# Moving some swapped copies of h from SyncE's DMA queue to ScalarE's in an attention and gated-MLP kernel

## The chip, the cores and the metric

One NeuronCore of a Trainium2 chip runs the whole kernel. The metric is the device time of one launch in microseconds (us), the median of several runs. The engines are named as the profile names them: PE is TensorE, DVE is VectorE, ACT is ScalarE, POOL is GpSimd, SP is SyncE, which here only issues DMAs. A "q" behind a name (SPq) means the engine's instruction queue, as it waits or issues a DMA.

## The reference

```python
B, S, D, H, F = 1, 2048, 576, 32, 4608     # head size D // H = 18
xn = layernorm(x)
# attention
q, k, v = split_heads(xn @ wqkv)
p = softmax(q @ k.T * 18 ** -0.5)
s = (p @ v merged over the heads) @ wo
# gated MLP without a nonlinearity inside
h = (xn @ w_gate) * (xn @ w_up)
g = silu(h @ w_down)
out = x + s * g
```

All tensors are float32. Products that need accuracy are done on operands split into a high and a low part (float32r), hence three matmuls for one.

## The kernel before

The work has a first phase (layer norm, the projections to q, k and v, which go to DRAM scratch), a long main phase, and a last projection with `wo`. The main phase mixes two kinds of work on PE, in an order that a planner in the program writes out by hand when the kernel is built (`order`, lines 1089 to 1170); every engine then runs its own list in that fixed order.

- **Attention**, head after head, 64 items a head: `a_item` (line 581) makes a block of scores in PSUM bank `pa` (line 588) for the row maxima that DVE takes (line 590); `b_item` (line 614) makes a block of scores in bank `pb` (line 620), and ACT takes its exponential (line 622, `pt<-pb`). `pb` has two buffers, so a score matmul can only start when ACT has finished with the block two before it. `pv_group` (line 631) multiplies by v.
- **The gated MLP**, in 72 units. Unit u is a pair of 128 columns of the hidden size (q, of NF2 = 18 column groups) for one block of 512 rows (c, of 4 passes): u = 18 c + q. PE works in two streams r = 0, 1 that use half of the rows of the array each (lines 667 to 672). Stream 0 makes the up product, which ACT copies out (`us`, line 675); stream 1 makes the gate product, which DVE multiplies by it (line 682). ACT then writes the high part of h (`hs`, line 685) and POOL the low part (line 686). The weights `wgu` and `wd` are loaded raw in the first pass, split by ACT and POOL (lines 190, 191, 223, 224), and stored to scratch by SP (`swg` line 196, `swd` line 229), from which the later passes load them (lines 182, 217).
- **The down product** of unit u (line 712) runs while unit u + 1 is made. Each stream owns 64 partitions, but needs h from all 128, so `turn_round` (line 692) makes a second copy of h with the two halves of the partitions swapped: `hx`, by two DMAs of 512 KB each (line 702). `hx` has one buffer. For unit 0 the copies are issued right behind POOL's part of h (`gate_end`, line 688); for units 1 to 70 in `down_end` (line 750), when the down product of the unit before has read `hx` for the last time; for unit 71 in `gate_end`, in two pieces of two DMAs (`hxl`, 256 KB each), one behind each half of h.

At the last unit of a pass `x_block` (line 357) loads the next 512 rows of x (`xc<-sx`) from scratch. `load_ring` and `load_pair` (lines 244 to 248) bring the heads' q and k as `ring<-sqk` and `pair<-sqk`.

SP issues every DMA named so far, in program order; POOL issues a few others. The DMAs of the hardware queues signal their landing on eight semaphores (DMAHW0 to DMAHW7) that are handed out in turn, and a DMA waits, before it is issued, until the one that used its semaphore before it has landed. A waiting instruction at the head of a queue holds back what stands behind it.

Of the kernel before, what the change touches and what calls it, by code (L numbers as in the profile page):

```python
# [20 lines left out]
FT = mybir.dt.float32  # L21
# [19 lines left out]
def kernel(  # L41
# [10 lines left out]
    nc = tc.nc  # L52
# [7 lines left out]
    NF2 = F // 256  # L60
# [509 lines left out]
    with ExitStack() as mid:  # L570
# [88 lines left out]
        hs, us = {}, {}  # L659
        TERMS = [t for b in range(9) for t in ((b, b, 0), (9 + b, b, 0), (b, b, 1))]  # L660
        half = [slice(0, 64), slice(64, 128)]
# [15 lines left out]
        def gate_end(n, ps):  # L677
            u, j = divmod(n, 2)
            if j == 0:
                hs[u] = gp.tile([128, 2, 2, 512], FR, name="hs", bufs=2)  # L680
            h32 = us.pop(n)
            nc.vector.tensor_tensor(h32, ps, h32, op=OP.mult)  # L682
            g_get(n + 2)
            hj = hs[u][:, j]
            nc.scalar.activation(hj[:, 0, :], h32, AF.Copy)  # L685
            nc.gpsimd.tensor_tensor(hj[:, 1, :], h32, hj[:, 0, :].bitcast(FT), op=OP.subtract)  # L686
            if u == 0 and j or u == len(units) - 1:
                turn_round(u, j)

        hx = {}  # L690

        def turn_round(u, j):

            if u == len(units) - 1:
                if j == 0:
                    hx[u] = accp.tile([128, 2, 2, 512], FR, name="hxl", tag="acc")
                js = slice(j, j + 1)
            else:
                hx[u] = gp.tile([128, 2, 2, 512], FR, name="hx", bufs=1)
                js = slice(0, 2)  # L700
            for r in range(2):
                nc.sync.dma_start(hx[u][half[r], js].bitcast(FT), hs[u][half[1 - r], js].bitcast(FT))

        DTERMS = [(k, j, a, e) for k in range(2) for j in range(2) for a, e in ((0, 0), (0, 1), (1, 0))]

# [25 lines left out]
        def down_end(r, u, s, ps):  # L731
            c, q = units[u]
            cs = slice(r * HALF, (r + 1) * HALF)
            if q == 0 and c >= 2:
                ready(sdone, 4 * c - 8 + s)
            a = sums(4 * c + s)[:, cs]
            if q == 0:
                nc.vector.tensor_copy(a, ps[:, 0:HALF])
            else:
                nc.vector.tensor_tensor(a, a, ps[:, 0:HALF], op=OP.add)  # L740
            if q == NF2 - 1 and c < NCH - 1:
                seen[c, s] = seen.get((c, s), 0) + 1
                if seen[c, s] == 2:
                    silu_store(4 * c + s)
            if s == 3:
                seen[u] = seen.get(u, 0) + 1
                if seen[u] == 2:
                    d_get(u + 1)
                    if u + 1 < len(units) - 1:
                        turn_round(u + 1, 1)  # L750
# [540 lines left out]
```

## Time and profile before

| | us |
|---|---|
| median of 3 runs | 2593.03 |
| lowest and highest of them | 2589.69, 2594.57 |
| the profiled execution | 2593.24 |
| its span, first to last instruction | 2591.4 |
| PE busy | 2573.7 |
| DVE busy | 1918.9 |
| ACT busy | 1459.4 |
| POOL busy | 589.2 |

The profile is a trace of one execution. Times in its views count from the start of the span. In a row of the timeline the first number is the start, the second the length, in square brackets stands how long the engine had been idle before it and what ended that. In a list of waits stand who waited, for what, the sum, the number of times and the longest.

### The profile page before, as it was taken

What the parts mean: (1) busy time and instruction counts of PE and PEld (TensorE: products, weight loads), DVE (VectorE), ACT (ScalarE), POOL (GpSimd) and SP (SyncE); (2) the same over time, 40 slices, a digit from 0 to 9 for tenths busy, and PEclk for the clock granted to TensorE, in tenths of its full rate; (3) what the DMA queues carried; (4) which work ended last, traced back from release to release, by engine and by line L of the source; (5) the groups of instructions that cost most, each with busy time, mean ns of one, the idle gap of its engine ahead of it and who ended that gap; (6) DMA issues with size and microseconds to landing.
All of it is one profiled execution on the core that took longest, in us unless ns stands there. A gap on an engine that the chain in (4) does not pass through costs nothing.

```text
span 2591.4 us, 59097 instructions
## 1 busy us (share of the span) xinstructions
PE 2573.7 (99%) x24360; PEld 2106.9 (81%) x24360; DVE 1918.9 (74%) x3377; ACT 1459.4 (56%) x2688; POOL 589.2 (23%) x659
## 2 busy tenths in 40 slices
PE   8999999999999999999999999999999999999999
PEld 7899877787888888877888888877788888887779
DVE  6208777777778888877788788877788888777527
ACT  5222666666665555655555565655555565555561
POOL 3114444434421111111111111111111211111115
PEclk9999999999999999999999999999999999999999
DMA  7799989888885666665686556655675666665567
GB/s 240 227 277 276 269 225 225 231 214 228 220 200 178 179 180 178 169 181 158 178 193 174 173 163 184 180 159 173 171 195 153 175 183 175 173 177 169 154 181 253
DMA packets 195897, 504.57 MB, mean 195 GB/s; under 512 B 58112, under 2 KB 116352, under 8 KB 156588
## 3 DMA queue, kind: packets, MB, share of 16 engines
q1 hardware_dynamic: 185676, 489.05, 67.8%
q0 software_dynamic: 9952, 11.74, 1.7%
q8 instruction: 192, 3.15, 0.5%
q14 instruction: 77, 0.63, 0.1%
HBM read 312.21 MB, written 107.61 MB: 162 GB/s over the span
## 4 chain that ended last, share of the span: by engine, by line
PE 96%; DMA 1%; DVE 1%; SPq 0%; issue 0%; ACT 0%; POOL 0%; ACTq 0%; POOLq 0%; DVEq 0%
PE pg L670 35%; PE pg L631 17%; PE pg L712 16%; PE pa L588 12%; PE pb L620 9%; PE pg L395 2%; PE pa L341 2%; PE pb L341 2%; PE pg L1221 1%; PE pa L1221 1%; PE pb L1221 1%; DMA hx<-hs 0%; DMA ring<-sqk 0%; DMA xin<-in_A_x_dram 0%; DVE hl L345 0%
## 5 line engine op out<-in xcount | busy, mean ns | idle before, releaser
L590 DVE TENSOR_REDUCE mx<-pa 128x1 f32<-128x512 f32 x2048 | 1361.6, 684 | 159.1 <-PE pa L588 69.7
L622 ACT ACTIVATE pt<-pb 128x512 f32<-128x512 f32 x2048 | 1154.9, 597 | 564.1 <-PE pb L620 458.9
L670 PE MATMUL pg<-xc,wgu 64*128 64x512 f32 x7776 | 1396.7, 392 | 0.0
L670 PEld LDWEIGHTS pg<-xc,wgu 64*128 64x128 f32 x7776 | 1054.9, 186 | 50.4 <-DVE acc L740 0.2
L620 PE MATMUL pb<-pair,ring 56*128 56x512 f32 x2006 | 788.9, 399 | 0.9 <-DMA ring<-sqk 0.9
L588 PE MATMUL pa<-pair,ring 54*128 54x512 f32 x2001 | 784.7, 398 | 0.3 <-DVE mx L590 0.3
L712 PE MATMUL pg<-wd,hs 64*128 64x288 f32 x3408 | 537.2, 292 | 1.2 <-DVE acc L740 1.2
L712 PE MATMUL pg<-wd,hx 64*128 64x288 f32 x3408 | 528.7, 292 | 1.2 <-DMA hx<-hs 1.1
L712 PEld LDWEIGHTS pg<-wd,hs 64*128 64x128 f32 x3408 | 474.1, 186 | 6.0 <-DVE acc L740 1.9
L712 PEld LDWEIGHTS pg<-wd,hx 64*128 64x128 f32 x3408 | 468.0, 185 | 5.7 <-DMA hx<-hs 1.9
L631 PE MATMUL pg<-pt,vt 128*32 128x512 f32 x4096 | 454.8, 594 | 0.0
L686 POOL TENSOR_TENSOR hs<-us,hs 128x512 fp32r<-128x512 f32 x144 | 186.2, 1293 | 1129.8 <-ACT hs L685 1087.9
L588 PEld LDWEIGHTS pa<-pair,ring 54*128 54x128 f32 x2001 | 363.2, 184 | 82.5 <-issue 47.8
L620 PEld LDWEIGHTS pb<-pair,ring 56*128 56x128 f32 x2006 | 364.7, 184 | 12.0 <-ACT us L675 1.5
L631 PEld LDWEIGHTS pg<-pt,vt 128*32 128x32 f32 x4096 | 125.6, 110 | 284.4 <-issue 280.6
L637 DVE TENSOR_TENSOR oc<-oc,pg 128x512 f32<-128x512 f32 x69 | 47.4, 688 | 320.8 <-PE pg L631 320.6
L740 DVE TENSOR_TENSOR acc<-acc,pg 128x288 f32<-128x288 f32 x544 | 233.8, 443 | 27.1 <-PE pg L712 24.2
L685 ACT ACTIVATE hs<-us 128x512 fp32r<-128x512 f32 x144 | 91.0, 632 | 154.3 <-DVE us L682 152.9
L651 POOL DMA_DIRECT2D sot<-oc x124 | 64.1, 523 | 329.7 <-DVE oc L648 327.6
L610 POOL DMA_DIRECT2D pair<-mt x128 | 78.0, 615 | 225.9 <-DVE mt L605 223.8
L635 ACT ACTIVATE oc<-pg 128x512 f32<-128x512 f32 x32 | 19.2, 599 | 189.2 <-PE pg L631 189.2
L191 POOL TENSOR_TENSOR wgu<-wraw,wgu 128x384 fp32r<-128x384 f32 x108 | 108.3, 1015 | 76.0 <-ACT wgu L190 70.9
(130 smaller groups left out, 1376.8 us busy)
## 6 DMA issues: line engine op xcount, KB each, us to landing
wgu<-swg SPq DMA_DIRECT2D x102, 1152.0 KB
hx<-hs SPq DMA_DIRECT2D x142, 512.0 KB
wd<-swd SPq DMA_DIRECT2D x50, 1152.0 KB
swg<-wgu SPq DMA_DIRECT2D x36, 1152.0 KB
pair<-sqk SPq DMA_DIRECT2D x192, 144.0 KB
ring<-sqk SPq DMA_DIRECT2D x384, 72.0 KB
swd<-wd SPq DMA_DIRECT2D x18, 1152.0 KB
sqk<-hl SPq DMA_DIRECT2D x32, 512.0 KB
```

The costliest lines, as they stand in the source:

```text
L191: nc.gpsimd.tensor_tensor(w[:, 9 + b:12 + b, :], raw[:, b:b + 3, :], w[:, b:b + 3, :].bitcast(FT), op=OP.subtract)
L341: nc.tensor.matmul(p, wq[b, a], xcs[c][:, e, :], start=n == 0, stop=n == len(PAIRS) - 1)
L588: nc.tensor.matmul(p, q[rows, t * 128:(t + 1) * 128], k[rows, c * 512:(c + 1) * 512], start=True, stop=True)
L590: nc.vector.tensor_reduce(mx[h][:, t, c:c + 1], p, axis=AX.X, op=OP.max)
L620: nc.tensor.matmul(p, k[rows, t * 128:(t + 1) * 128], q[rows, c * 512:(c + 1) * 512], start=True, stop=True)
L622: nc.scalar.activation(pt[t, c], p, AF.Exp, scale=scale)
L631: nc.tensor.matmul(p[32 * c:32 * c + 32, :], vt[h // 2][:, t, 6 * (h % 2):6 * (h % 2) + 32], pt[t, c], start=t == ts[0], stop=t == ts[-1])
L670: nc.tensor.matmul(ps, gw[n][half[r], a, :], xg[i][half[r], e, :], start=k == 0, stop=k == len(TERMS) - 1)
L685: nc.scalar.activation(hj[:, 0, :], h32, AF.Copy)
L686: nc.gpsimd.tensor_tensor(hj[:, 1, :], h32, hj[:, 0, :].bitcast(FT), op=OP.subtract)
L712: nc.tensor.matmul(ps[:, 0:HALF], (hx if k else hs)[u][half[r], j, a, s * 128:(s + 1) * 128], dw[u][half[r], k, j, e, :], start=n == 0, st ...
L740: nc.vector.tensor_tensor(a, a, ps[:, 0:HALF], op=OP.add)
```

## The change

The two DMAs of `turn_round` are issued on ACT's queue, and not on SP's, for units 0 to 3 and for those units whose place in a pass is the first or the last: 17, 18, 35, 36, 53, 54 and 71 (u % 18 is 0 or 17). That is eleven units and 24 DMAs of 146. Nothing else is edited.

```diff
             for r in range(2):
-                nc.sync.dma_start(hx[u][half[r], js].bitcast(FT), hs[u][half[1 - r], js].bitcast(FT))
+                (nc.scalar if u < 4 or u % NF2 in (0, NF2 - 1) else nc.sync).dma_start(hx[u][half[r], js].bitcast(FT), hs[u][half[1 - r], js].bitcast(FT))
```

PE, DVE and POOL run the same lists as before. Three places on ACT and SP follow, with the semaphores that each instruction waits for; a number behind a name (PE_49) is that of the build. First ACT, before, in unit 3, around 287 us of the profile (`draw` is the raw down weight that becomes `wd`):

```order
L622 ACTIVATE pt<-pb 128x512 [waits PE_49] x2
L223 ACTIVATE wd<-draw 128x2x288 [waits DMAHW3_49,DMAHW2_49,DMAHW5_49,PE_49,Pool_49]
L622 ACTIVATE pt<-pb 128x512 [waits PE_49]
L223 ACTIVATE wd<-draw 128x2x288 [waits DMAHW6_49,DMAHW4_49]
L622 ACTIVATE pt<-pb 128x512 [waits PE_49] x4
```

The same place with the change:

```order
L622 ACTIVATE pt<-pb 128x512 [waits PE_49] x2
L702 DMA hx<-hs 64x2048 [waits DMAHW6_49,DMAHW1_49,DMAHW7_49,PE_49,Pool_49]
L702 DMA hx<-hs 64x2048 [waits DMAHW2_49]
L223 ACTIVATE wd<-draw 128x2x288 [waits DMAHW5_49,DMAHW3_49]
L622 ACTIVATE pt<-pb 128x512 [waits PE_49]
L223 ACTIVATE wd<-draw 128x2x288 [waits DMAHW6_49,DMAHW4_49]
L622 ACTIVATE pt<-pb 128x512 [waits PE_49] x4
```

The pair of DMAs has come to stand ahead of a split of weights and of an exponential.

Next SP with the change, in unit 17, around 746 us: the last loads of x for the next pass (`xc`) and the first of the ring loads that follow them.

```order
L364 DMA xc<-sx 64x1024 [waits DMAHW0_49,PE_49]
L364 DMA xc<-sx 64x1024 [waits DMAHW1_49,PE_49]
L364 DMA xc<-sx 64x1024 [waits DMAHW2_49,PE_49]
L242 DMA ring<-sqk 18x1024 [waits DMAHW3_49]
L242 DMA ring<-sqk 18x1024 [waits DMAHW4_49]
```

ACT at the same place, with the change:

```order
L622 ACTIVATE pt<-pb 128x512 [waits PE_49] x12
L702 DMA hx<-hs 64x2048 [waits DMAHW5_49,DMAHW1_49,DMAHW6_49,PE_49,Pool_49]
L702 DMA hx<-hs 64x2048 [waits DMAHW2_49]
L223 ACTIVATE wd<-draw 128x2x288 [waits DMAHW7_49,DMAHW0_49]
L622 ACTIVATE pt<-pb 128x512 [waits PE_49] x2
```

The copies stood between the `xc` and the ring loads on SP, and are now on ACT with the semaphores DMAHW1 and DMAHW2, which the last two `xc` loads used before them.

Last ACT in unit 71, around 2498 us, with the change:

```order
L685 ACTIVATE hs<-us 128x512 [waits DMAHW2_49,DMAHW1_49,DVE_49]
L702 DMA hxl<-hs 64x1024 [waits DMAHW4_49,Pool_49]
L702 DMA hxl<-hs 64x1024 [waits DMAHW5_49]
L622 ACTIVATE pt<-pb 128x512 [waits PE_49] x8
L675 ACTIVATE us<-pg 128x512 [waits PE_49]
```

Behind ACT's half of h stands now the copy, which waits for POOL's half (Pool_49), and behind that eight exponentials.

The changed program's semaphores give, for each moved pair, the DMAs that must have landed before it is issued, by the turn of the eight:

| unit | first DMA waits for | second DMA waits for |
|---|---|---|
| 0 | `sv<-vo`, long before | `swg<-wgu`, the one before the last |
| 1 | the second of three ring loads | the third of them |
| 2 | the third of three ring loads | the third of three `pair<-sqk` |
| 3 | the first of three `pair<-sqk` | the `swg<-wgu` behind these |
| 17 | the last `xc` load but one | the last `xc` load |
| 18 | a `wgu<-swg` of the unit before | the first of three `pair<-sqk` |
| 35 | the last `xc` load but four | the last `xc` load but two |
| 36 | the second of three `pair<-sqk` | a `wgu<-swg` of the unit before |
| 53 | an `xc` load in the middle | the last `xc` load but five |
| 54 | the last ring load of an earlier group | a `wgu<-swg` of the unit before |
| 71, first half | a ring load of an earlier unit | the next ring load |
| 71, second half | the first half's second DMA | the first `wor<-in_A_wo_dram` |

## The prediction

> **What bounds the kernel now.** I read the page's busy times first, then who PE waits for, then the rows of the copies themselves, and last the timeline at each place where a copy moves.
>
> ```profile
> PE 2573.7 (99%) x24360; PEld 2106.9 (81%) x24360; DVE 1918.9 (74%) x3377; ACT 1459.4 (56%) x2688; POOL 589.2 (23%) x659
> PE pg L712 <- DMA hx<-hs: 1.1, 1, 1.1
> PE pb L620 <- DMA ring<-sqk: 0.9, 1, 0.9
> PEld pg L712 <- DMA hx<-hs: 1.9, 2, 1.5
> L702 SPq DMA_DIRECT2D hx<-hs x142: 467/587/5686, 219.2 to 2483.7; - x142
> L622 ACT ACTIVATE pt<-pb 128x512 f32<-128x512 f32 x2048 | 1154.9, 597 | 564.1 <-PE pb L620 458.9 <-PE pa L588 63.0 <-PE pg L670 16.3
> ```
>
> PE is busy 2573.7 of 2591.4 us, so it sets the end, and what is to be won by earlier copies is what PE loses to them. That is little: its weight loads lose 1.9 us to `hx` in the whole stretch of the first units (the 1.1 us of its matmuls lies inside that), and 0.9 us to a ring load in unit 17, which on SP stands behind the copy of that unit. All gains together are 2.8 us, about 0.1% of the time.
>
> ACT has room on average (56%), but it has a strict order, and its exponentials hand PSUM back to PE. With two `pb` buffers an exponential that ends late by more than the gap to the second next score matmul stops PE, and PE, being busy to 99%, cannot win that back. So each moved pair has to be asked: when does ACT get to go on, and which score matmul is waiting then?
>
> **The change part by part.** A pair of copies holds SP for 1.10 to 1.12 us when nothing else delays it (rows below at 2499.45, 783.57 and 748.90). There is no DMA from ACT in the trace; I take the same 1.1 us for a pair on ACT, some 0.6 us for its second DMA. From below the bound is nothing, from above the 5.7 us of the longest row of L702.
>
> *Unit 71.* The copy stands behind POOL's half of h, which only begins when ACT has ended its half.
>
> ```profile
> 2497.41 0.63 ACT L685 ACTIVATE hs<-us 128x512 fp32r<-128x512 f32 x1 [0.64 <-DVE us L682]
> 2498.12 1.30 POOL L686 TENSOR_TENSOR hs<-us,hs 128x512 fp32r<-128x512 f32 x1 [19.70 <-ACT hs L685]
> 2497.95 2.28 ACT L622 ACTIVATE pt<-pb 128x512 f32<-128x512 f32 x4
> 2498.71 0.39 PE L620 MATMUL pb<-ring,pair 56*128 56x512 f32 x1
> 2499.45 1.10 SPq L702 DMA_DIRECT2D hxl<-hs  x2
> 2509.81 0.39 PE L620 MATMUL pb<-ring,pair 56*128 56x512 f32 x1
> 2510.46 1.10 SPq L702 DMA_DIRECT2D hxl<-hs  x2
> ```
>
> On SP that wait costs nobody. On ACT the exponential that began at 2497.95 comes after the pair: 2499.45 + 1.10 + 0.60 = 2501.15 is its end, and the score matmul that needs its buffer, at 2498.71 before, starts at about 2501.2: **+2.5**. The second half of h repeats it: 2510.46 + 1.10 + 0.60 = 2512.2 against 2509.81, about 2512.3: **+2.5**. Nothing covers these; POOL was idle before, so its 1.30 us cannot come sooner.
>
> *Unit 17.* ACT reaches the pair at about 749, just after the last reading of `hx`, when SP issued it too. But by the table of semaphores the pair waits for the last two `xc` loads.
>
> ```profile
> 745.31 1.54 SPq L364 DMA_DIRECT2D xc<-sx  x2
> 748.90 1.12 SPq L702 DMA_DIRECT2D hx<-hs  x2
> 750.07 5.75 SPq L242 DMA_DIRECT2D ring<-sqk  x6
> 749.03 0.68 ACT L223 ACTIVATE wd<-draw 128x576 fp32r<-128x576 f32 x1
> 749.60 0.59 ACT L622 ACTIVATE pt<-pb 128x512 f32<-128x512 f32 x1
> 750.93 0.39 PE L620 MATMUL pb<-pair,ring 56*128 56x512 f32 x1
> 1334.03 0.45 SPq L364 DMA_DIRECT2D xc<-sx  x1
> 1343.13 0.48 SPq L702 DMA_DIRECT2D hx<-hs  x1
> SPq L702 <- DMA xc<-sx: 0.8, 1, 0.8
> 745.00:756.00 11.00, 11.00 (x106) 10.96 (x104) 10.75 (x21) 9.35 (x18) 5.32 (x6) 1.00 1.06 210
> ```
>
> How long such a load takes is seen in unit 35: the copy at 1343.13 had waited for the `xc` load issued at 1334.03, 9.1 us. The last two of unit 17 were issued at 745.3 and about 746.4, so they land near 754.4 and 755.5. The second copy then goes at 755.5 to 756.1, the split of weights takes the next 0.57 (749.03 to 749.60 before), the exponential 0.6: it ends at 757.3, and the score matmul of 750.93 starts at 757.4, **+6.5**. The ring loads no longer stand behind the copy and have these microseconds besides, so the 0.9 us that PE waited for them is gone: **+5.6** in all. From below: eight loads of 256 KB in flight, 2.1 MB, at the 286 GB/s that the row of unit 3 below shows in place of 210 here take 7.3 us, which makes it +3.8; from above +7.
>
> *Units 0 to 3.* The rows of unit 3 first, with the stretch from 283 to 292 us, whose last columns are PE's clock, the DMA engines' share and the GB/s, and then ACT's idle times in units 0 and 1:
>
> ```profile
> SPq L196 <- DMA swd<-wd: 2.8, 1, 2.8
> 283.30 0.34 SPq L196 DMA_DIRECT2D swg<-wgu  x1
> 283.00:292.00 9.00, 9.00 (x98) 8.86 (x96) 7.38 (x14) 6.33 (x12) 5.29 (x5) 1.00 1.02 286
> 287.54 0.69 ACT L223 ACTIVATE wd<-draw 128x576 fp32r<-128x576 f32 x1
> 288.13 0.58 ACT L622 ACTIVATE pt<-pb 128x512 f32<-128x512 f32 x1
> 290.60 0.39 PE L620 MATMUL pb<-pair,ring 56*128 56x512 f32 x1
> 221.68 0.60 ACT L675 ACTIVATE us<-pg 128x512 f32<-128x512 f32 x1 [2.54 <-PE pg L670]
> 244.52 0.60 ACT L675 ACTIVATE us<-pg 128x512 f32<-128x512 f32 x1 [2.08 <-PE pg L670]
> 263.14 1.09 ACT L622 ACTIVATE pt<-pb 128x512 f32<-128x512 f32 x2
> ```
>
> In units 0 and 1 no exponential runs yet (the first is at 263.14), and ACT idles 2.54 and 2.08 us before its next due work: POOL's 1.3 and 1.1 us of issue in unit 0, 1.1 in unit 1 fit into it. Zero. In unit 3 the second copy waits for the `swg` store issued at 283.30, when `swd` had landed. Ahead of its end stand four `draw` of 144 KB, three `pair` of 144 KB and its own 1152 KB: 2.2 MB, at 286 GB/s 7.7 us, so it lands at 291.0. The DMA engines are full there (share 1.02), so I leave that landing where it was, though a copy of 1 MB has changed queues. The second copy goes at 291.0 to 291.6, split 0.6, exponential 0.6: it ends at 292.8, and the score matmul of 290.60 starts at about 292.9, **+2.3**. Because this is fixed by a landing and not by PE, the 1.9 us that PE no longer waits in unit 2, and any loss there behind a `pair` load, are inside it and not added. Bounds: 0, if the store lands by 288.5, to +4.5.
>
> *Units 35, 18, 36, 53, 54.* In unit 35 the second copy cannot go before 1343.13 on ACT either.
>
> ```profile
> 1341.81 0.60 ACT L622 ACTIVATE pt<-pb 128x512 f32<-128x512 f32 x1 [0.39 <-PE pb L620]
> 1343.66 0.39 PE L620 MATMUL pb<-pair,ring 56*128 56x512 f32 x1
> 783.57 1.12 SPq L702 DMA_DIRECT2D hx<-hs  x2
> 785.67 0.39 PE L620 MATMUL pb<-pair,ring 56*128 56x512 f32 x1
> 1373.39 1.11 SPq L702 DMA_DIRECT2D hx<-hs  x2
> 1375.48 0.39 PE L620 MATMUL pb<-pair,ring 56*128 56x512 f32 x1
> 1938.66 0.60 ACT L622 ACTIVATE pt<-pb 128x512 f32<-128x512 f32 x1 [7.03 <-PE pb L620]
> 1972.67 1.09 ACT L622 ACTIVATE pt<-pb 128x512 f32<-128x512 f32 x2 [2.14 <-PE pg L670]
> ```
>
> 1343.13 + 0.48 + 0.60 = 1344.2, the matmul of 1343.66 starts at 1344.3: **+0.7**. In units 18 and 36 the exponential behind the pair ends at 783.57 + 1.12 + 0.60 = 785.3 and 1373.39 + 1.11 + 0.60 = 1375.1, before 785.67 and 1375.48; in 53 and 54 ACT idles 7.03 and 2.14 us. Zero, and up to 0.5 each if a pair takes ACT half as long again.
>
> The sum: 5.0 + 5.6 + 2.3 + 0.7 = **+13.6 us** on the profiled execution's 2593.24, that is **2606.8**. That execution lies 0.2 us above the median of the runs shown, so I take 2607.
>
> [...]
>
> **The rivals.**
>
> *Not slower: the wait does not hold ACT's computing.* If a DMA that waits on ACT's queue lets the exponentials behind it pass, only the removed waits count: 1.9 and 0.9, so 2590.4. For it: the trace has no DMA on ACT. Against it: on SP the wait does hold the queue (the copy at 1343.13 waited 0.8 us and nothing was issued past it). [...]
>
> *About as before: what a pair waits for lands early.* SP is freed of 24 DMAs and could issue the `xc` loads and the store sooner. Then unit 17 costs only its issue (748.90 + 1.12 + 0.57 + 0.60 = 751.2 against 750.93, +0.4, less 0.9), unit 3 gives its 1.9 us back, unit 35 nothing, and unit 71 its 5.0: +2.6, or 2595.8. Against it: no copy stands ahead of the `xc` loads of unit 17 on SP, and in unit 3 the DMA engines are full.
>
> *Slower still: the issue itself is held.* SP's longest copy held its queue for 5.7 us in the crowded first units. If ACT's is held like this once, at unit 3, the term there grows by about 5.1, to 2611.9; the point from which this decides is an issue of more than 1.1 us on ACT.
>
> **How the numbers follow.** The sum as worked out has 0.67, the held issue 0.13, early landings 0.12, a wait that does not hold ACT 0.08. The low ends of the terms (3.8 for unit 17, 0 for unit 3, 0.3 for unit 35, and 2.8 for unit 71 if the issue costs nothing) make +6.9, or 2600; the high ends (7, 4.5, 1.0, 6 and 2 for the pairs counted as zero) +20.5, or 2614, where the held issue lies too. For 8 in 10 I take 2599 to 2613. Less than 0.2%, 5.2 us, cannot be told from no change here. Faster by that needs more than all that PE waits for these DMAs: 0.02. Within it fall most of the early landings (0.10) and of the last rival (0.06): 0.16. Slower: 0.82.
>
> **What the changed profile would show.** Right: idle PE in front of a score matmul (L620) that waits for ACT's `pt`, about 6 us in one piece near 751, 2 near 291, and 2.5 twice near the end; ACT idle there with `xc`, `swg` and POOL's `hs` named; the waits of PE for `hx` and for the ring load gone. Wrong: exponentials that run on while a copy waits, a pair of copies on ACT far from 1.1 us, or `xc` landing near 750 in unit 17. The prediction fails by more than its range if PE stops at units 18, 36, 53 or 54, or if the stop of unit 17 is not there.

## The result, and the profile after

The changed kernel takes 2612.87 us (median of 4 runs, 2611.95 to 2614.33), against 2593.8 us for the kernel before beside it: a ratio of 1.008, with a 95% interval of 1.0068 to 1.0092. It is slower by about 20 us. The prediction said 2607, with a range up to 2613: the median lies 0.1 us inside that end, and 1.008 times the 2593.03 us shown before lies 0.8 us above it. The profiled execution took 2612.0 us with a span of 2609.8, which is 18.4 more than the 2591.4 before. The prediction's sum was made against the profiled execution of before, and was 13.6.

The page of the changed kernel, its busy times and its new DMA queue, ACT's (packets, MB, share of the 16 DMA engines):

```profile
PE 2578.5 (99%) x24360; PEld 2109.1 (81%) x24360; DVE 1919.7 (74%) x3377; ACT 1458.0 (56%) x2688; POOL 589.4 (23%) x659
...
q10 hardware_dynamic: 1920, 11.54, 2.0%
```

The busy times of ACT and POOL are those of before within 1.4 us, and so is that of DVE. PE's grew by 4.8 us although it does the same matmuls. The rest of the 18.4 us must be idle time, and the list of waits says for whom: first PE, then ACT.

```profile
PE pb L620 <- ACT pt L622: 15.3, 5, 6.4
...
ACT wd L223 <- DMA ring<-sqk: 7.3, 1, 7.3
...
ACT wd L223 <- DMA swg<-wgu: 6.0, 1, 6.0
...
ACT pt L622 <- issue: 5.1, 2, 2.6
```

PE waits five times for an exponential, 15.3 us in all; before there was no such row, while PE's rows for `hx` (1.1) and for the ring load (0.9) have gone. ACT's own waits stand at the instruction *behind* the copies: the split of weights (L223) in units 3 and 17, the exponential (L622) in unit 71. In the row of 7.3 us the profile names a ring load as the last releaser. By the trace's landings it was the last two `xc` loads that held the pair: they landed at 758.40 and 759.91, and the copies went at 758.55 and 759.93. Unit 3, then 17, 35 and 71:

```profile
290.74 0.47 ACTq L702 DMA_DIRECT2D hx<-hs  x1
291.31 0.68 ACT L223 ACTIVATE wd<-draw 128x576 fp32r<-128x576 f32 x1 [5.98 <-DMA swg<-wgu]
292.54 0.79 PE L620 MATMUL pb<-pair,ring 56*128 56x512 f32 x1 [3.84 <-ACT pt L622]
...
752.14 1.10 ACT L622 ACTIVATE pt<-pb 128x512 f32<-128x512 f32 x2 [0.16 <-PE pb L620]
758.55 1.85 ACTq L702 DMA_DIRECT2D hx<-hs  x2
760.50 0.68 ACT L223 ACTIVATE wd<-draw 128x576 fp32r<-128x576 f32 x1 [7.26 <-DMA ring<-sqk]
761.72 0.79 PE L620 MATMUL pb<-pair,ring 56*128 56x512 f32 x1 [6.44 <-ACT pt L622]
773.87 0.39 PE L620 MATMUL pb<-pair,ring 56*128 56x512 f32 x1
774.79 0.39 PE L620 MATMUL pb<-pair,ring 56*128 56x512 f32 x1
1355.82 0.50 PE L620 MATMUL pb<-pair,ring 56*128 56x512 f32 x1 [0.30 <-ACT pt L622]
2511.59 1.12 ACTq L702 DMA_DIRECT2D hxl<-hs  x2
2512.76 2.27 ACT L622 ACTIVATE pt<-pb 128x512 f32<-128x512 f32 x4 [2.55 <-issue]
2513.41 0.50 PE L620 MATMUL pb<-ring,pair 56*128 56x512 f32 x1 [2.38 <-ACT pt L622]
2527.14 0.50 PE L620 MATMUL pb<-ring,pair 56*128 56x512 f32 x1 [2.32 <-ACT pt L622]
```

Three rows of before that have not been shown, the partners of those at 752.14, 773.87 and 774.79:

```profile
748.03 1.10 ACT L622 ACTIVATE pt<-pb 128x512 f32<-128x512 f32 x2 [0.16 <-PE pb L620]
761.41 0.39 PE L620 MATMUL pb<-pair,ring 56*128 56x512 f32 x1
763.45 0.47 PE L620 MATMUL pb<-pair,ring 56*128 56x512 f32 x1 [0.92 <-DMA ring<-sqk]
```

The place of a loss is found by setting the start of one instruction in the two traces against each other, from stop to stop. In unit 3 the matmul of 290.60 now starts at 292.54, +1.94; but by 752 the gap is 752.14 - 748.03 = +4.11, with no stop in between. In unit 17 it becomes 761.72 - 750.93 = +10.79 at the stop, and 773.87 - 761.41 = +12.46 some ten microseconds later, again with no stop. So PE loses time *behind* its two long stops, while it is busy. The view by stretches tells how, in steps of 3.413 us (columns: length; busy time and count of PE, PEld, DVE, ACT, POOL; PE's granted clock; DMA share; GB/s):

```profile
287.33:290.74 3.41, 1.36 (x11) 0.77 (x9) 1.38 (x2) 0.00 (x0) 0.00 (x0) 1.00 1.15 267
290.74:294.16 3.42, 1.62 (x8) 1.35 (x10) 0.00 (x0) 2.71 (x5) 2.03 (x2) 0.50 1.02 300
294.16:297.57 3.41, 3.41 (x20) 2.67 (x18) 1.38 (x2) 0.97 (x2) 0.76 (x1) 0.50 1.03 333
...
754.95:758.37 3.42, 0.33 (x4) 0.00 (x0) 0.99 (x2) 0.00 (x0) 0.00 (x0) 1.00 0.73 135
758.37:761.78 3.41, 0.06 (x2) 0.06 (x2) 0.00 (x0) 1.28 (x3) 0.46 (x1) 0.50 0.95 171
761.78:765.20 3.42, 3.42 (x16) 2.72 (x18) 1.17 (x2) 2.03 (x4) 2.37 (x2) 0.50 0.99 178
765.20:768.61 3.41, 3.41 (x32) 2.91 (x32) 3.06 (x6) 2.53 (x5) 0.00 (x0) 1.00 0.33 74
```

From within both stops on, PE's granted clock is 0.50, for two such steps each: in the full step at 761.78 PE gets 16 matmuls done, in the next one at the full clock 32. Before, the clock was 1.00 at both places. The stops of unit 71, 2.4 and 2.3 us, left it at 1.00 in this execution.

### The profile page after: what moved, and what is told of

It is laid out like the page before. It is cut to its first block, busy times and chain, and to the rows that moved or that the text cites. A ratio compares the mean times of both kernels' runs of the same rounds, so it can differ in the third digit from the quotient of the medians.

```text
span 2609.8 us, 59075 instructions
## 1 busy us (share of the span) xinstructions
PE 2578.5 (99%) x24360; PEld 2109.1 (81%) x24360; DVE 1919.7 (74%) x3377; ACT 1458.0 (56%) x2688; POOL 589.4 (23%) x659
## 4 chain that ended last, share of the span: by engine, by line
PE 93%; DMA 3%; DVE 1%; issue 1%; SPq 0%; POOL 0%; ACT 0%; ACTq 0%; POOLq 0%; DVEq 0%
PE pg L670 34%; PE pg L631 17%; PE pg L712 15%; PE pa L588 11%; PE pb L620 9%; PE pg L395 2%; PE pa L341 2%; PE pb L341 2%; PE pg L1221 1%; DMA xc<-sx 1%; DMA o<-sot 1%; DMA swd<-wd 0%; PE pa L1221 0%; PE pb L1221 0%; DMA draw<-in_B_w_down_dram 0%
## 5 line engine op out<-in xcount | busy, mean ns | idle before, releaser
L622 ACT ACTIVATE pt<-pb 128x512 f32<-128x512 f32 x2048 | 1153.8, 597 | 568.3 <-PE pb L620 471.9
```

The lines of the kernel that those rows point to most:

```text
L622: nc.scalar.activation(pt[t, c], p, AF.Exp, scale=scale)
```

## The experiments

The theory after the result: a copy on ACT's queue holds the exponentials behind it for its wait and its issue, PE stops when they come late, and a stop that is long enough also costs PE half its clock for some microseconds. The rivals: the moved copies cost by contention, wherever they are; the clock fell for a reason of its own; the issue itself was held. Differences in us are between medians; the ratio with its 95% interval is a separate estimate, and can differ from that of the medians by 0.04%. In every kernel below, what is not named is as before; "(...)" and "..." in the edits stand for lines and arguments left out. The runs of the kernel before beside them have medians of 2591.8 to 2592.2 us (2589.9 to 2596.7). Where a kernel has lines added, the copies stand at L709, the score matmul at L621 and the exponential at L623 (L624 in the kernel of repeated exponentials). The costs of the four kernels that take the change apart (units 71, 17, 3, and those priced at nothing; +8.0, +9.2, +5.8 and +3.1 us) add up to 26 us even without unit 35, more than the change's 19 to 20, so these medians are not the prices of the places inside the change.

### Unit 71 alone

```diff
-                nc.sync.dma_start(...)
+                (nc.scalar if u in (71,) else nc.sync).dma_start(...)
```

> Only the four copies of unit 71 go to ACT, the rest as before. Theory (ACT's list is held by a copy's wait and issue, and PE stops for the late exponentials; after a stop that is long enough PE's clock is halved for some microseconds): two stops of 2.3 to 2.6 us at L620, +5 us in all, no record of a half clock before the end of the program. Rival (contention: each moved copy costs the same share of the 18.4 us, 0.77 us each, wherever it is): +3.1 us, spread out, no stops.

Median 2599.83 us (2596.67 to 2602.49), ratio 1.0028 (1.0019 to 1.0037). PE's stops in the timeline of this kernel:

```profile
764.42 0.46 PE L620 MATMUL pb<-pair,ring 56*128 56x512 f32 x1 [2.04 <-DMA ring<-sqk]
...
2503.92 0.49 PE L620 MATMUL pb<-ring,pair 56*128 56x512 f32 x1 [2.39 <-ACT pt L622]
2517.61 0.50 PE L620 MATMUL pb<-ring,pair 56*128 56x512 f32 x1 [2.31 <-ACT pt L622]
```

The two stops of unit 71 are there as expected, 2503.92 - 2498.71 = +5.2 and then 2517.61 - 2509.81 = +7.8; of the +5.2, 2.5 had been there since unit 17, where nothing was moved: PE waited 2.04 us for the ring load, 0.92 before, and a record of half clock from 765.45 to 768.87 follows. So "no half clock" was wrong, and the moved copies account for 5.3 us of this execution. The fastest of the ten, 2596.67, is 4.9 above before's median, as the two stops alone would make it; the median is 8.0 above, and whether the wait in unit 17 makes the rest in the other executions is not shown. Contention shared out over the copies (+3.1, no stops) does not fit.

### Unit 17 alone

```diff
-                nc.sync.dma_start(...)
+                (nc.scalar if u in (17,) else nc.sync).dma_start(...)
```

> Only the two copies of unit 17 go to ACT. Theory: one stop of about 6.4 us at L620 in unit 17, PE's wait for the ring load (0.9 us before) gone, and one record of a half clock right after the stop that costs 1 to 3 us: +6.5 to +8.5 us. If the clock has nothing to do with the stop, +5.6 and no such record. Contention: +1.5 us.

Median 2601.05 us (2599.64 to 2601.80), ratio 1.0032 (1.0020 to 1.0044): +9.2, above the expected +6.5 to +8.5. The stop:

```profile
757.78 0.79 PE L620 MATMUL pb<-pair,ring 56*128 56x512 f32 x1 [7.73 <-ACT pt L622]
```

It is 1.3 us longer than in the change; the second copy went at 756.0, as the last `xc` load allowed. The half clock holds for 10.24 us from 752.90 here, three steps of 3.413. Both parts of the theory stand; contention (+1.5) does not.

### Unit 3 alone

```diff
-                nc.sync.dma_start(...)
+                (nc.scalar if u in (3,) else nc.sync).dma_start(...)
```

> Only the two copies of unit 3 go to ACT; units 0 to 2 stay on SP, so the 1.9 us that PE waits for hx in unit 2 remain. Theory: the second copy is bound to the landing of the swg store near 291, and not to PE, so the shift behind the stop is about the +2.4 us that the change had there (from its -0.5 at the start to +1.9), with a stop of some 2 us between before's times instead of 4; a half clock after it only if the stop covers enough of a clock step: +2 to +4 us. If the landing moves with the work, +4 to +6. Contention: +1.5 us.

Median 2597.64 us (2594.64 to 2600.69), ratio 1.0020 (1.0011 to 1.0030): +5.8, beyond the +2 to +4. In the profiled execution, 2597.06 us, the stop is where the landing puts it:

```profile
291.91 0.50 PE L620 MATMUL pb<-pair,ring 56*128 56x512 f32 x1 [2.29 <-ACT pt L622]
```

291.91 - 290.60 = +1.3, close to the change's +1.94 although unit 2's copies came 5 us later here: the landing sets it, not PE. By the trace's landings the `swg` store landed at 290.09 and the second copy went at 290.11 (290.72 and 290.74 in the change). A record of half clock follows, 3.41 us from 292.54. This execution's span is 3.9 us above before's, inside the +2 to +4. The median agrees with the +4 to +6 of the other reading, that the landing moves with the work, but the landing here does not bear that out; the executions differ by 6 us, and where the slower ones lose more is open.

### The units that were priced at nothing

```diff
-                nc.sync.dma_start(...)
+                (nc.scalar if u in (0, 1, 2, 18, 36, 53, 54) else nc.sync).dma_start(...)
```

> The copies of units 0, 1, 2, 18, 36, 53 and 54 go to ACT, 14 of the change's 24, all those whose waits the theory prices at nothing. Theory: no stop anywhere, PE's 1.9 us of waiting for hx in unit 2 gone, no half clock: -1 to -2.5 us. Contention: 14 x 0.77 = +10.8 us. If the half clock came from the DMAs on ACT and not from the stops, a record of it near 290.

Median 2594.88 us (2592.64 to 2598.85), ratio 1.0013 (1.0004 to 1.0023): +3.1, where the theory said -1 to -2.5. Contention as stated (+10.8) is out too. The profiled execution was the fastest of the ten and had no half clock. PE no longer waits for `hx` in unit 2, but ACT waits, and PE for it:

```profile
273.89 1.35 ACT L190 ACTIVATE wgu<-wraw 128x384 fp32r<-128x384 f32 x3 [3.02 <-DMA wraw<-in_B_w_gate_dram]
275.78 0.49 PE L620 MATMUL pb<-pair,ring 56*128 56x512 f32 x1 [1.31 <-ACT pt L622]
```

The same split of raw weights in the trace before:

```profile
270.80 1.34 ACT L190 ACTIVATE wgu<-wraw 128x384 fp32r<-128x384 f32 x3
```

It stood 3 us earlier and waited for nothing. The copies of unit 2 now leave at 261 and 263, not at 266 and 269, and the load of `wraw` beside them, issued at 260.7 here and at 260.5 before, lands at 273.8 and not at 269.3 (both from the traces' DMA events). So in this execution what PE wins at `hx` it loses at the next score matmul. Being the fastest, it does not show what makes the median slower. Two runs take this apart.

### Unit 2 alone, and the same without unit 2

```diff
-                nc.sync.dma_start(...)
+                (nc.scalar if u in (2,) else nc.sync).dma_start(...)
```

> Only the two copies of unit 2 go to ACT. Theory after e4_zero (a second mechanism, contention: the copies go 5 us earlier and share the DMA engines with the raw weights wraw; ACT's split of them, L190, waits for the later landing, and the exponentials behind the split stop PE): the 1.9 us won at hx are given back at a score matmul near 276 that waits for ACT, -1 to +4 us with a wide spread between executions, and the longer stops followed by a half clock. Rival (e4's +3 us come from the later units 18 to 54): -1.9 us, and no stop near 276.

Median 2593.80 us (2592.16 to 2600.07), ratio 1.0007 (0.9997 to 1.0016), with the stop again:

```profile
275.83 0.50 PE L620 MATMUL pb<-pair,ring 56*128 56x512 f32 x1 [1.44 <-ACT pt L622]
```

The gain of 1.9 us is not there, and the spread is wide. The `wraw` load was issued at 260.5, as before, and landed at 273.8 again: with unit 2 alone moved, it is unit 2's copies that delay it. The median is 1.6 above before's, and the interval includes no change.

```diff
-                nc.sync.dma_start(...)
+                (nc.scalar if u in (0, 1, 18, 36, 53, 54) else nc.sync).dma_start(...)
```

> The copies of units 0, 1, 18, 36, 53 and 54 go to ACT, e4_zero without unit 2. Theory: within 1 us of before, as the sum of the prediction had these units, and as narrow a spread as before's. Rival (the later units cost e4's +3 us): +3 us and the wide spread.

Median 2595.48 us (2590.53 to 2598.83), ratio 1.0010 (1.0001 to 1.0020): +3.3, which is the rival's answer. One place is unit 18. First the rows of the timeline there, then the copies' row in the view of `hx` (shortest, median and longest issue in ns):

```profile
784.41 3.14 ACTq L702 DMA_DIRECT2D hx<-hs  x2
...
788.25 0.50 PE L620 MATMUL pb<-pair,ring 56*128 56x512 f32 x1 [1.43 <-ACT pt L622]
```

```profile
L702 ACTq DMA_DIRECT2D hx<-hs x12: 468/490/2635, 218.2 to 1974.3; - x12
```

The second copy waited for no landing (the `pair` load that it is bound to had landed at 781.65); its issue itself lasted 2.64 us. That is the prediction's third rival, at another place. In the profiled execution of the change the longest issue on ACT was 1.16 us. In this execution, whose span is 4.2 us above before's, PE's wait for the ring load of unit 17, on SP, was 1.2 us longer, and in unit 71, where nothing was moved, a down product waited 1.37 us for DVE (0.10 before). So unit 18 makes less than half of the 4.2 here; how far the copies on ACT's queue add to the other two, and what makes the median, these runs do not tell.

### Unit 17 later

```diff
+        held, LATE = [], {17: 6}
...
             nc.scalar.activation(pt[t, c], p, AF.Exp, scale=scale)
+            for g in list(held):
+                g[0] -= 1
+                if not g[0]:
+                    held.remove(g)
+                    g[1]()
...
-                nc.sync.dma_start(...)
+                def copy(..., eng=nc.scalar if u in (17,) else nc.sync):
+                    eng.dma_start(...)
+                if u in LATE:
+                    held.append([LATE[u], copy])
+                else:
+                    copy()
```

> As e2_17, the copies of unit 17 alone on ACT, but issued six exponentials later, with the same DMAs waited for. Theory (the cost of unit 17 is that ACT's list stands behind the landing of the last xc loads, near 755): ACT now comes to the pair at about 756, when these have landed, so nothing waits but for the issue of 1.1 us; the stop of 6.4 us becomes 1 us or less, no half clock, and the ring loads still gain: -1 to +1 us. Rival (the copies cost their time by being on ACT's queue): +9 as e2_17.

Median 2592.11 us (2591.21 to 2593.92), ratio 0.9998 (0.9989 to 1.0007): 9 us less than with the same copies six exponentials earlier, on the same queue. The place, by the timeline and by stretches:

```profile
754.07 2.28 ACTq L709 DMA_DIRECT2D hx<-hs  x2
755.90 0.73 PE L676 MATMUL pg<-xc,wgu 64*128 64x512 f32 x3 [0.65 <-DMA xc<-sx]
756.40 1.09 ACT L623 ACTIVATE pt<-pb 128x512 f32<-128x512 f32 x2 [3.25 <-DMA xc<-sx]
757.05 0.71 PE L621 MATMUL pb<-pair,ring 56*128 56x512 f32 x1 [0.42 <-ACT pt L623]
```

```profile
753.75:757.16 3.41, 2.08 (x16) 1.08 (x16) 1.93 (x4) 0.76 (x2) 0.00 (x0) 1.00 0.88 180
757.16:760.58 3.42, 3.42 (x18) 2.68 (x20) 2.14 (x4) 2.27 (x5) 0.86 (x1) 0.50 1.03 214
```

The stop of 6.44 us has shrunk to 0.42. It was the wait ahead of the exponentials, not the queue. ACT still comes too early, at about 752.5 and not at 756, and idles 3.25 us for `xc`, but six more exponentials are done by then, and PE stops only briefly. One step of half clock follows, which the expectation had excluded, and PE itself waits 0.65 us for `xc`; with the gain at the ring load that comes out at nothing.

### The stop alone

```diff
+        AGAIN = {400 + 50 * j: (5, 8, 11, 14)[j % 4] for j in range(24)}
...
-            nc.scalar.activation(pt[t, c], p, AF.Exp, scale=scale)
+            for _ in range(1 + AGAIN.get(64 * h + i, 0)):
+                nc.scalar.activation(pt[t, c], p, AF.Exp, scale=scale)
```

> The kernel before, with no copy on ACT, and with the exponential repeated on the spot at 24 places of the long run: 5, 8, 11 and 14 times more, by turns, each 0.57 us, which stops PE for some 2.3, 4.0, 5.7 and 7.4 us six times each. Theory (the stop alone halves the clock): records of a half clock behind most of the stops of 5.7 and 7.4 us, on a grid of 3.413 us, behind few of 4 us and none of 2.3. Rival (the clock fell because of the DMAs on ACT): no record at all before the end.

One run, 2750.29 us, span 2748.5. There are 20 records of half clock ahead of the program's end, none of them near a DMA on ACT, for there is none. The trace of before has none ahead of its end either, so the clock falls here because PE stops. From PE's list of waits, and three stops of 1.85, 3.87 and 1.40 us by stretches:

```profile
PE pb L621 <- ACT pt L624: 109.7, 22, 8.5
```

```profile
1201.28:1204.69 3.41, 1.56 (x13) 1.09 (x11) 1.94 (x3) 3.28 (x7) 0.00 (x0) 1.00 1.03 251
1204.69:1208.10 3.41, 3.41 (x18) 2.75 (x16) 1.27 (x2) 1.88 (x5) 0.00 (x0) 0.50 0.42 91
...
1750.82:1754.24 3.42, 2.03 (x17) 1.39 (x13) 2.71 (x4) 3.05 (x6) 0.00 (x0) 1.00 1.07 262
1754.24:1757.65 3.41, 0.93 (x6) 0.48 (x6) 0.00 (x0) 3.31 (x7) 0.00 (x0) 1.00 0.28 58
1696.21:1699.62 3.41, 2.12 (x28) 2.12 (x30) 1.96 (x5) 3.25 (x6) 1.09 (x1) 1.00 0.90 308
```

The guess about the size was wrong: stops of 1.9 to 2.7 us did it as well, four times. What tells these stops apart is how busy PE was in one step of 3.413 us: 1.56 us of the step at 1201.28 brought the half clock in the next; 2.03 at 1750.82 did not, 0.93 in the step after it did (a record of 3.41 us from 1757.65); 2.12 at 1696.21 brought none. The span is 157.1 us longer than before's; PE waited some 111 of them, and the other 46 over 20 records make about 2.3 us a record. That is the price of the clock: PE is busy for 90.7 us of the 39 steps at half clock, and half of 90.7 is 45.4.

### Unit 71 later

```diff
+        held, LATE = [], {71: 3}
...
-                nc.sync.dma_start(...)
+                def copy(..., eng=nc.scalar if u in (71,) else nc.sync):
```

The rest of the edit is as for unit 17.

> As e1_71, the four copies of unit 71 alone on ACT, but each pair three exponentials later, so that POOL has ended its half of h when ACT comes to the pair. Theory: POOL's 1.3 us no longer stand on ACT's list; what is left are the two issues of 1.1 us, a stop of 0.7 us or less at each: the shift at the end of unit 71 +0.5 to +1.5 us against e1's +5.2. Rival (the issue, not the wait for POOL, made e1's stops): +4 to +5 us there again.

Median 2594.70 us (2592.56 to 2596.38), ratio 1.0007 (0.9998 to 1.0017), 5.1 us less than with the copies at their place in the change. PE's stops:

```profile
2501.84 0.50 PE L621 MATMUL pb<-ring,pair 56*128 56x512 f32 x1 [0.56 <-ACT pt L623]
2513.68 0.50 PE L621 MATMUL pb<-pair,ring 56*128 56x512 f32 x1 [0.59 <-ACT pt L623]
```

0.56 and 0.59 against 2.39 and 2.31: the wait for POOL's half of h made most of the stop, the issue of the pair, 1.15 us, the rest. Set against before, the starts of PE's matmuls lag by 0.6 us ahead of unit 71's stops and by 2.1 behind them, +1.5, the upper end of what was expected.

### All copies on ACT

```diff
-                nc.sync.dma_start(...)
+                nc.scalar.dma_start(...)
```

> All 146 copies on ACT. It measures the issue: theory (most issues take ACT 0.47 to 0.6 us, some are held, as one of 2.6 us in e6_no2): median of L702's row on ACT 0.5 us, longest 2 to 6 us, a few of the 146 above 1.2 us. Rival (a held issue is SP's alone, or comes from its longer list): none above 1.2 us. The time: slower than the change, since now 71 units pay for issue and waits; at 0.5 to 3 us a unit +30 to +200 us.

One run, 2632.44 us, 40 above before. The copies' row in the view of `hx`:

```profile
L702 ACTq DMA_DIRECT2D hx<-hs x142: 467/469/2357, 218.6 to 2515.5; - x142
```

Of the 146 issues 8 lasted over 1.2 us, the longest 2.36. On SP before it was also 8 of 146, the longest 5.69. So a held issue is no property of SP; one in twenty is held on ACT too. What holds it is open: seven of the eight on ACT lie beside the issue of a DMA on SP, but the 2.64 us in unit 18 above and SP's eight of before had no other engine's issue beside them.

### The change with unit 17 later

```diff
+        held, LATE = [], {17: 6}
...
-                nc.sync.dma_start(...)
+                def copy(..., eng=nc.scalar if u in (0, 1, 2, 3, 17, 18, 35, 36, 53, 54, 71) else nc.sync):
```

> The whole change, but with the copies of unit 17 issued six exponentials later, as in e7_17late. Theory: it loses the change's stop of 6.4 us there and most of the half clock behind it, 5 to 8 us: 2605 to 2608 us, ratio to before 1.005. If the terms of the places don't add (what is won at 17 is lost later), 2610 to 2613.

Median 2604.84 us (2604.33 to 2608.83), ratio 1.0053 (1.0040 to 1.0067): 8.0 us below the change, or 6.4 when each is set against the kernel before beside it; the change's trace lost 7.3 us at that place. In the profiled execution one of unit 71's stops, 2.38 us as in the change, did bring a half clock:

```profile
2502.29:2505.70 3.41, 1.03 (x10) 0.61 (x8) 0.00 (x0) 0.90 (x2) 1.28 (x1) 1.00 0.92 362
2505.70:2509.11 3.41, 3.41 (x18) 2.59 (x18) 0.00 (x0) 1.84 (x4) 0.00 (x0) 0.50 0.60 141
```

The same stop fell into one step here, and across two in the change. At unit 3 it was the other way round: a stop of 3.27 us fell across two steps and left the clock at 1.00. In unit 36 an issue held for 2.16 us made a stop of 1.01 us.

### Unit 17 later, on SP

```diff
+        held, LATE = [], {17: 10}
...
-                nc.sync.dma_start(...)
+                def copy(..., eng=nc.scalar if u in () else nc.sync):
```

> The kernel before, all copies on SP, with those of unit 17 ten exponentials later, so that the six ring loads and a weight load go ahead of them; the only use of the change's idea that is left, since PE waits there for the ring load. Theory: PE's wait for the ring load in unit 17 (0.9 us in before, up to 2.0 in other executions) is gone and hx still lands ahead of its first use near 771: -0.5 to -2 us, ratio 0.9992 to 0.9998, hardly to be told from no change. Rival: the copies come too late, and PE waits at 771: +1 to +4 us.

Median 2590.70 us (2589.53 to 2595.42), ratio 0.9998 (0.9989 to 1.0007). That cannot be told from no change, so no version that beats the kernel before was found. The profiled execution was the slowest of its eleven, 2595.42; in it PE waited 2.75 us for `hx` in unit 2, where nothing was changed, and the clock fell behind it (1.01 us of the step at 276.45, then 0.50). The kernel before has that weak place too.

## Why the prediction came out too small

The sum, term by term, with the differences of start times from the rows above and those of the prediction:

| term | predicted | measured |
|---|---|---|
| unit 3, stop (with unit 2's gain in it) | +2.3 | 292.54 - 290.60 = +1.9 |
| half clock behind it | not in the sum | 752.14 - 748.03 = 4.11, so +2.2 |
| unit 17, stop | +6.5 | 761.72 - 750.93 = 10.79, so +6.7 |
| half clock behind it | not in the sum | 773.87 - 761.41 = 12.46, so +1.7 |
| ring load no longer waited for | -0.9 | 774.79 - 763.45 = 11.34, so -1.1 |
| unit 35 | +0.7 | 1355.82 - 1343.66 = 12.16, so +0.8 |
| unit 71, first half | +2.5 | 2513.41 - 2498.71 = 14.70, so +2.5 |
| unit 71, second half | +2.5 | 2527.14 - 2509.81 = 17.33, so +2.6 |
| behind unit 71 | not in the sum | 18.4 - 17.33 = +1.1 |
| sum | +13.6 | +18.4 |

**The waits and their sizes held.** The terms that the prediction had add up to 13.5 us in the trace, against 13.6; none is off by more than 0.4, so that is not a matter of errors that cancel. The stop of unit 17 was there because of the last two `xc` loads, as the table of semaphores said, and goes when the pair is issued later; that of unit 71 stood behind POOL's half of h, and shrinks to 0.6 us when the pair comes three exponentials later; that of unit 3 is bound to the `swg` store, whose landing let the second copy go 0.02 us later in two traces. A pair of issues on ACT took 1.12 us in unit 71, the 1.1 that was taken over from SP.

**The step that failed is the sum itself: it priced a stop of PE at its own length.** "It ends at 757.3, and the score matmul of 750.93 starts at 757.4, **+6.5**" takes PE to go on as fast as before, and so puts at nothing, without a reason, what PE does behind the stop. It goes on at half its clock (0.50 in the stretches shown). The two records behind the stops of units 3 and 17 cost 3.8 us (half of the 8.5 us that PE is busy in their four steps would be 4.3), and the experiment with the repeated exponentials shows that a stop alone brings them. Of the remaining 1.1 us behind unit 71, 0.4 came in the last projection, by PE's last matmuls (2586.54 before, 2604.22 now, +17.7); the other 0.7 fall behind PE's last work, and their cause is open.

**The range's upper end was built from the terms' high ends alone** (7, 4.5, 1.0, 6 and 2, which give 2614; the range was taken to 2613) and had no room for a cost that follows each long stop.

**"Zero" for units 0, 1, 2, 18, 36, 53 and 54** was right for the profiled execution of the change, where PE has no stop at any of them. As a median it was not: these units alone cost 3.1 us. The traces show a late `wraw` load in unit 2 and an issue held for 2.6 us in unit 18; that these make the whole of the 3.1 is not shown. The gain of 1.9 us in unit 2 was swallowed by unit 3 in the change, as the prediction said; alone it is given back at the weights' split.

**The rivals.** A wait that lets ACT compute on is refuted by the first waits of ACT shown above, 5.98 and 7.26 us. Early landings: the last `xc` loads freed the pair at 758.4 and 759.9, 4 us behind the predicted 754.4 and 755.5 because everything there ran 4 us later: they were issued at 749.82 and 751.06, and took 8.6 and 8.8 us where 9.1 had been assumed. They did not land early. The held issue is real (2.64 us in unit 18 without unit 2, up to 2.36 with all copies on ACT), but in the profiled execution of the change the longest, 1.16 us, stood in unit 1, where PE has no stop.

## What to carry to other kernels

A DMA on the queue of an engine that computes was here an instruction in that engine's order (ACT stood idle 5.98 and 7.26 us behind such copies): before moving it there, find what it has to wait for, and put it behind that point; six exponentials later made 9 us into nothing. A stop of the matmul engine has to be priced with what its clock does next, here about 2 us more (2.2 and 1.7 in the change, 2.3 with the repeated exponentials) for each stop that leaves a step of 3.4 us less than 47% busy. A transfer that is made earlier can push another one back (with unit 2's copies 5 us earlier, `wraw` landed at 273.8 and not at 269.3), so a wait removed is not yet a gain.

## What the runs showed of the hardware

**The clock followed PE's work in the step before.** The records of the clock change on a grid of 3.413 us: in the change's trace at 290.74, 297.57, 758.37 and 765.20, which are 2, 135 and 2 such steps apart. I took every such step between 215 and 2560 us in ten of the traces (before, after, the three single units, the two with unit 17 later on ACT, the one on SP, all copies on ACT, and the repeated exponentials), with PE's busy share. At the full clock, all 30 steps in which PE was busy for less than 47% were followed by a step at half clock; of the 40 with 48 to 80% one was, that of 61% shown for the later unit 17; why that one was, the traces do not show. At half clock, a step with less than 75% was followed by another at half clock (25 of 25), and one with more than 90% by the full clock (31 of 31). So one and the same stop of unit 71 (2.39 us in the change, 2.38 with unit 17 later) cost nothing beyond its length where it fell across two steps, and some 1.5 us more where it fell into one: with unit 17 later, the lag behind before grew by 4.15 us from unit 71's first stop to its second, and by 2.63 in the change. A step need not be idle to bring the half clock: the one at 1201.28 above was 46% busy.

**The issue of a copy on ACT** took 0.47 us in the median, in the change and with all copies on ACT; in the change 23 of 24 took 0.61 at most, and with all copies on ACT 8 of 146 took over 1.2 us. What makes up such a row, no run here shows.
